# Thresholded attention with a gated mix: transposed weights copied by ScalarE or VectorE, rooms counted at creation, new due offsets

## The chip, the cores and the metric

One core of one Trainium2 chip runs the whole program. The metric is device time in microseconds (us), from start to end of one execution; lower is better. Engines are named as in the profile: PE is TensorE's matrix multiply and PEld its weight load, DVE is VectorE, ACT is ScalarE, POOL is GpSimd, SP is SyncE, which issues the DMAs.

## The reference

```
scores = q @ k.T / sqrt(64)                     # 8 batches, 8 heads, 576 x 576
keep   = scores >= max(scores, row) - tau       # tau = 0.02
attn   = exp(scores - max) where kept, else 0
attn   = attn / (sum(attn, row) + 1e-9)
x      = attn @ v, heads side by side           # 8 x 576 x 512
gate   = sigmoid(causal convolution of x, 5 taps for each channel)
out    = (gate * (x @ w_val)) @ w_out           # 512 x 512 each
```

Everything is float32. The three projection weights arrive as 64-bit words, which the kernel turns into float32 at its start.

## The kernel before

The work is cut into 32 units, one for each batch and pair of heads; four units make a batch. A unit has nine score tiles of 128 rows. In code and profile:

- **Scores** (S, L594): PE multiplies q and k into a PSUM room `u`. There are four rooms, each two banks wide, and everything that PE writes goes into one of them.
- **Row minimum** (L601): DVE scales the scores into `sb` and finds the row's extreme `nm`. It frees the PSUM room of the scores.
- **Threshold** (L609, L611), then **exp** (L619) on ACT into `e`, then **keep** (L636) on DVE, which multiplies by the mask into `pp` and sums the row. The planner can choose another way: ACT makes a steep ramp (L617) and a second exp with the sum (L630), and DVE adds 1e-9 to the sum (L656). This spares DVE the keep.
- **Reciprocal** (L657) and its spreading over 128 columns (`inv`, L665 on ACT or L667 on POOL).
- **Transposes** (T, L724): PE turns `pp` and `inv` against `ident` into a PSUM room: eight pieces (512 columns) for a group's first head, and ten and two of `inv` (768 columns) for the second. The 64 rows that are left of each head form a group of their own, `pl`.
- **Copy** (L736): the turned weights go from PSUM to `T` in SBUF, 512 or 768 columns; this frees the room. In the kernel before only ACT does it. The copies of `pl` (L740, L744) are ACT's in both kernels.
- **Attend** (C, L797; L768 in the first five units): 40 matmuls of `T` with `v`, and DVE divides them into `xT` (L774, L806).
- **Convolution** (L859, L864), **gate** (L889), and the parts of `xT` whose sum is the float32 value (`xh`, `xl`).
- **Products** (P, L955): in 16 runs of 24 matmuls a batch, 8 for `w_val` and 8 for `w_out`, after all four units of the batch. Between the two runs of a product ACT reads two numbers (`seen`, L943). The results leave by L993 (DVE) and L1057 (DVE) or L1059 (ACT).

No order is written out by hand. While the program is built, `carry_out` plans it. Each operation has an engine (or some that it may choose from), a cost in us, a due time, what it waits for and what rooms it takes. The planner takes the engine on which something can begin first, and there the operation with the smallest due time; that is then the order of the instructions in each engine's queue, which the chip carries out strictly from front to back. A due time is the number of the tile plus an offset from a table: `EARLY` before tile 69, `AT` after it. `PACE_M` is the distance in due time of one product run from the next. `FREE` names the operations that may go to a second engine from tile 69 on.

A room is a buffer in turn. `Rooms` keeps two lists: `times`, the planner's book of when rooms come free, and `free`, the buffers that are handed out when the planned instructions are emitted. The first unit takes one buffer of `pp` and one of `pl` already while the operations are being set up (`load_at_once`, L489), by `take`, which shortens `free` alone.

```
        def take(self):
            return self.free.pop(0)[1]
```

The choice between engines is a list of ways (`either`, L140). In the kernel before the copy is written with no second way in force, since `FREE` doesn't hold `copy`:

```
                    [] if self.both else either(
                        k, "copy", ("DVE", moved(m * P), moved(m * P) + 0.14, self.copy(c0, m, nc.vector.tensor_copy))
                    ),
```

Of the kernel before, what the change touches and what calls it, by code (L numbers as in the profile page):

```python
# [19 lines left out]
PACE_M = 2.32187  # L20
# [8 lines left out]
MERGED = 0.17  # L29
AT_ONCE = 4  # L30
# [3 lines left out]
for x in range(6):  # L34
# [9 lines left out]
    inv=2,  # L44
# [6 lines left out]
    swap=1421.79, fetch_q=-40.66, score=724.17, largest=2786.67, lowest=-2765.51,  # L51
    weigh=-6117.15, keep=1522.46, add=80.1, inv=-1623.91, divide=-1008.91, turn=-3930.93,
    copy=862.76, attend=-3114.29, evac=992.12, fetch=1723.48, high_k=-882.65, low_k=8.36,
    scale_q=3700.52, high_q=607.44, low_q=504.1, place=-1721.2, copies=1191.3, copies_q=1475.29,
    fetch_v=-167.12, prep=-27.65, early1=1435.43, early2=486.5, early3=169.93,
    conv_high=-4198.07, tap0=1991.9, conv_low=7462.8, tap=1501.34, tap_step=-6371.23,
    gate=-331.54, products=737.92, val=512.47, g_high=2207.99, g_low=4141.22, out=3582.59,
    send=724.8, words=-4.76, words_step=7.01, words_fetch=0.77, split=35.72, words_sub=-25.09,
    words2=-1.91, cw=-6.65, corner=-6.73,
# [3 lines left out]
    swap=-3308.32, fetch_q=-1710.45, score=-200.07, largest=2077.61, lowest=7991.15,  # L63
    weigh=-5989.81, keep=-497.79, add=34.01, inv=-769.95, divide=699.66, turn=-4372.54,
    copy=-1133.49, attend=-844.28, evac=-2380.24, fetch=1474.15, high_k=-1420.92, low_k=1798.23,
    scale_q=809.97, high_q=21.29, low_q=-257.02, place=1138.28, copies=2504.1, copies_q=3020.69,
    fetch_v=-2736.64, prep=-4.29, early1=15.1, early2=13.7, early3=23.08, conv_high=-526.99,
    tap0=3714, conv_low=5082.45, tap=-2747.74, tap_step=-4329.15, gate=839.2, products=737.34,
    val=-3061.81, g_high=1852.92, g_low=1584.46, out=-922.38, send=-3484.92, words=561.36,
    words_step=236.07, words_fetch=1847.17, split=-1153.58, words_sub=-721.5, words2=-332.82,  # L70
    cw=-3820.12, corner=3365.88,
# [3 lines left out]
FREE = ('conv_high', 'low_q', 'out')  # L75
# [3 lines left out]
def tile_thresholded_attention_gated_mix(  # L79
# [84 lines left out]
    class Rooms:  # L164
# [6 lines left out]
        def take(self):  # L171
            return self.free.pop(0)[1]
# [9 lines left out]
    shape = [0]  # L182
    wire = [1.2]
# [29 lines left out]
    def carry_out():  # L213
        done_ops = []
        while True:
            best = None
            for e, ops in open_ops.items():
# [7 lines left out]
                if can:  # L225
                    t = min(x for x, _ in can)
                    o = min((x[1] for x in can if x[0] <= t), key=lambda o: o.due)
                    if best is None or (t, o.due) < (best[0], best[1].due):
                        best = (t, o, e)
# [964 lines left out]
```

## Time and profile before

| what | value |
| --- | --- |
| median of 3 runs | 698.6 us (697.45 to 698.98) |
| the profiled execution | 697.67 us, its span 695.9 us |
| PE busy | 664.3 us, 95% of the span |
| DVE busy | 596.1 us, 86% |
| ACT busy | 587.4 us, 84% |
| POOL busy | 249.5 us, 36% |

Three stretches are to be told apart. Until about 147 us the weights are being converted beside the first units. From there to 657 us the program repeats itself with each batch: scores, transposes and attend of one batch, with the products of the batch before it in between. From 657 us on PE has little but the last batch's products. Busy shares over the whole span mix the three. A matmul's record ends where a model puts it, and matmuls overlap, so that a short wait can hide within PE's busy time: the distance from the start of one piece to the start of the next tells more than its length.

### The profile page before, as it was taken

What the parts mean: (1) busy time and instruction counts of PE and PEld (TensorE: products, weight loads), DVE (VectorE), ACT (ScalarE), POOL (GpSimd) and SP (SyncE); (2) the same over time, 40 slices, a digit from 0 to 9 for tenths busy, and PEclk for the clock granted to TensorE, in tenths of its full rate; (3) what the DMA queues carried; (4) which work ended last, traced back from release to release, by engine and by line L of the source; (5) the groups of instructions that cost most, each with busy time, mean ns of one, the idle gap of its engine ahead of it and who ended that gap; (6) DMA issues with size and microseconds to landing.
All of it is one profiled execution on the core that took longest, in us unless ns stands there. A gap on an engine that the chain in (4) does not pass through costs nothing.

```text
span 695.9 us, 21477 instructions
## 1 busy us (share of the span) xinstructions
PE 664.3 (95%) x8610; PEld 521.8 (75%) x8610; DVE 596.1 (86%) x1598; ACT 587.4 (84%) x1206; POOL 249.5 (36%) x404
## 2 busy tenths in 40 slices
PE   8877889999999999999999999999999999999997
PEld 5544557667887777888787788877778887777897
DVE  6988989998888898988979989888989889799642
ACT  6998989999889988998879989799889988799620
POOL 2554555673222620433222422226214332224231
PEclk9999999999999999999999999999999999999999
DMA  7123333023321233223222233311332232220102
GB/s 266 51 96 108 123 116 103 33 70 117 118 87 29 78 120 102 84 86 103 64 94 86 68 120 103 103 40 66 120 106 82 85 104 75 83 86 1 53 19 70
DMA packets 21076, 61.19 MB, mean 88 GB/s; under 512 B 2928, under 2 KB 4336, under 8 KB 20976
## 3 DMA queue, kind: packets, MB, share of 16 engines
q1 hardware_dynamic: 20832, 59.62, 25.3%
q8 instruction: 68, 1.11, 0.7%
q14 instruction: 32, 0.26, 0.1%
q10 hardware_dynamic: 144, 0.20, 0.1%
HBM read 50.37 MB, written 9.44 MB: 86 GB/s over the span
## 4 chain that ended last, share of the span: by engine, by line
PE 53%; DVE 27%; ACT 13%; issue 6%; DMA 0%; DVEq 0%; ACTq 0%
PE u L955 19%; PE u L797 14%; DVE sb L601 12%; PE u L594 11%; DVE pp L636 8%; PE u L724 7%; ACT e L619 3%; ACT T L736 3%; ACT pp L630 3%; PE u L768 2%; ACT e L617 2%; DVE pre L864 2%; DVE r L657 1%; DVE pl L636 1%; ACT inv L665 1%
## 5 line engine op out<-in xcount | busy, mean ns | idle before, releaser
L601 DVE TENSOR_SCALAR_CACHE_REDUCE sb<-u,sc 128x576 f32<-128x576 f32 x288 | 228.0, 809 | 26.2 <-PE u L594 13.9
L594 PE MATMUL u<-k,q 64*128 64x288 f32 x1240 | 190.0, 418 | 5.1 <-DVE sb L601 3.3
L736 ACT COPY T<-u 128x512 f32<-128x512 f32 (+1 forms) x256 | 169.9, 688 | 13.2 <-PE u L724 12.4
L636 DVE SCALAR_TENSOR_TENSOR pp<-sb,th,e 128x577 f32<-128x577 f32 x164 | 145.0, 892 | 16.1 <-ACT e L619 15.3
L619 ACT ACTIVATE e<-sb,nm 128x576 f32<-128x576 f32 x193 | 146.6, 772 | 3.5 <-DVE sb L601 1.3
L797 PE MATMUL u<-T,v 128*64 128x256 f32 (+1 forms) x1080 | 136.9, 408 | 2.0 <-ACT T L736 2.0
L724 PEld LDWEIGHTS u<-ident,pp 64*128 64x128 f32 x2304 | 102.8, 139 | 46.1 <-ACT T L736 9.8
L594 PEld LDWEIGHTS u<-k,q 64*128 64x128 f32 x1240 | 108.4, 187 | 29.5 <-DVE sb L601 8.9
L724 PE MATMUL u<-ident,pp 64*128 64x64 f32 x2304 | 114.7, 226 | 15.3 <-DVE sb L601 7.8
L797 PEld LDWEIGHTS u<-T,v 128*64 128x64 f32 x1080 | 75.1, 137 | 54.4 <-ACT T L736 3.1
L864 DVE SCALAR_TENSOR_TENSOR pre<-xT,cw,pre 128x576 f32<-128x576 f32 x121 | 107.7, 890 | 1.7 <-POOL pre L859 0.9
L955 PE MATMUL u<-xh,wvh 64*128 64x288 f32 x512 | 87.3, 326 | 0.9 <-ACT seen L943 0.3
L955 PE MATMUL u<-gh,woh 64*128 64x288 f32 x512 | 84.1, 316 | 0.9 <-ACT T L744 0.6
L617 ACT ACTIVATE e<-sb,th 128x576 f32<-128x576 f32 x95 | 73.3, 775 | 8.0 <-DVE th L611 5.3
L955 PE MATMUL u<-xh,wvl 64*128 64x288 f32 x512 | 78.7, 291 | 0.0
L955 PE MATMUL u<-xl,wvh 64*128 64x288 f32 x512 | 78.6, 291 | 0.0
L955 PE MATMUL u<-gh,wol 64*128 64x288 f32 x512 | 77.9, 291 | 0.0
L955 PE MATMUL u<-gl,woh 64*128 64x288 f32 x512 | 77.9, 291 | 0.0
L630 ACT ACTIVATE pp<-e,minus 128x576 f32<-128x576 f32 x92 | 71.2, 774 | 0.7 <-DVE pp L636 0.2
L1024 POOL TENSOR_TENSOR gl<-g,gh 128x288 fp32r<-128x288 f32 x64 | 58.9, 935 | 31.8 <-ACT gh L1016 31.6
L667 POOL TENSOR_SCALAR inv<-r 128x128 f32<-128x128 f32 x79 | 25.0, 316 | 123.8 <-DVE r L657 106.1
L955 PEld LDWEIGHTS u<-xh,wvh 64*128 64x128 f32 x512 | 51.1, 185 | 6.4 <-DVE xT L806 3.3
(92 smaller groups left out, 992.7 us busy)
## 6 DMA issues: line engine op xcount, KB each, us to landing
q<-qT SPq DMA_DIRECT2D x31, 608.0 KB, 4.1
k<-kT SPq DMA_DIRECT2D x31, 496.0 KB, 5.0
v<-vs SPq DMA_DIRECT2D x32, 320.0 KB, 2.9
outT<-o SPq DMA_DIRECT2D x28, 288.0 KB, 2.2
pre<-w_val SPq DMA_DIRECT2D x4, 512.0 KB, 6.9
pre<-w_out SPq DMA_DIRECT2D x4, 512.0 KB, 3.5
outT<-o SPq DMA_DIRECT2D x8, 144.0 KB, 1.8
pp<-first SPq DMA_DIRECT2D x2, 192.0 KB, 3.0
```

The costliest lines, as they stand in the source:

```text
L594: nc.tensor.matmul(row(self.s)[:, a, :], t.q[rows, x : x + P], t.k[rows, k0 : k0 + HS], start=i == 0, stop=h is not None or i == 1, skip_g ...
L601: nc.vector.tensor_scalar(self.sb[:, :S].rearrange("p (a f) -> p a f", a=2), row(self.room()), sc, None, op0=ALU.mult, op1=ALU.min, accum_ ...
L617: nc.scalar.activation(y, x, AF.Prelu, bias=self.th, scale=-1.0, alpha=STEEP)
L619: nc.scalar.activation(y, x, AF.Exp, bias=self.nm, scale=-1.0)
L630: nc.scalar.activation(grp.p[:, i * S : (i + 1) * S], self.e[:, :S], AF.Exp, bias=minus, accum_out=grp.sums[:, i : i + 1])
L636: nc.vector.scalar_tensor_tensor(grp.p[:, i * S : (i + 1) * S + 1], self.sb, self.th, self.e, op0=ALU.is_le, op1=ALU.mult, accum_out=grp.s ...
L724: nc.tensor.transpose(tp[:, r, i * APART_BY : i * APART_BY + D], x[rows, :], ident[rows, rows])
L736: engine(T[:, c0 : c0 + n, self.off : self.off + P].rearrange("p c (r q) -> p r c q", r=2), tp)
L797: nc.tensor.matmul(a[hs, : W[half.j]], t.v[:, c0 : c0 + D], half.T[:, 2 * NKC if c == NKC else h * NKC + c, 0 : W[half.j]], start=c == 0, ...
L864: engine.scalar_tensor_tensor(cv, pair.xT[:, i + a : i + z], cw[:, g, i : i + 1], cv, op0=ALU.mult, op1=ALU.add)
L955: nc.tensor.matmul(made["room"][:, to, 0:HS], wt[rows, c, e * P : (e + 1) * P], moving(c, i)[rows, parts[j]], start=turn == c == n == 0, s ...
L1024: engine.tensor_sub(gs[e][1][:, c], g[x][:, c], gs[e][0][:, c].bitcast(F32))
```

## The change

`take` now also shortens `times` when it is called before the planned instructions are emitted, so that the planner knows of three rooms of `pp` and one of `pl` instead of four and two. `FREE` holds `copy`, so that each copy of 512 or 768 columns from tile 69 on goes to ACT or DVE, as the planner finds; `low_q`, which it loses, names nothing in this kernel. The due offsets in `AT` and `EARLY` and `PACE_M` are other numbers. `AVOID`, a weight on the cost of going from one kind of matmul to another, is 0.0 and changes nothing.

```
-PACE_M = 2.32187
+PACE_M = 2.20003
+AVOID = 0.0
 AT = dict(
-    copy=862.76, attend=-3114.29, evac=992.12, fetch=1723.48, high_k=-882.65, low_k=8.36,
+    copy=1463.16, attend=-2397.28, evac=2111.21, fetch=2756.29, high_k=-882.65, low_k=8.36,
...
-FREE = ('conv_high', 'low_q', 'out')
+FREE = ('conv_high', 'out', 'copy')
...
         def take(self):
+            if not emitting:
+                self.times.pop(0)
             return self.free.pop(0)[1]
...
+    emitting = []
...
-                    o = min((x[1] for x in can if x[0] <= t), key=lambda o: o.due)
+                    o = min((x[1] for x in can if x[0] <= t), key=(lambda o: o.due + AVOID * CHANGE.get((shape[0], o.shape), 0.0)) if e == "PE" else lambda o: o.due)
...
+        emitting.append(True)
         for o, emit in done_ops:
```

Counted over the program, the planned instructions that change their number are these:

| instruction | engine | before | after |
| --- | --- | --- | --- |
| copy of 512 columns, L736 | ACT | 128 | 76 |
| copy of 768 columns, L736 | ACT | 128 | 88 |
| copy of 512 columns | DVE | 0 | 52 |
| copy of 768 columns | DVE | 0 | 40 |
| keep, L636 | DVE | 193 | 143 |
| second exp, L630 | ACT | 95 | 145 |
| 1e-9 to the sum, L656 | DVE | 77 | 115 |
| `inv`, L665 | ACT | 81 | 45 |
| `inv`, L667 | POOL | 79 | 115 |
| result, 576 columns, L1057 / L1059 | DVE / ACT | 7 / 21 | 12 / 16 |
| threshold, L611 / L609 | DVE / ACT | 113 / 101 | 121 / 106 |

PE has the same matmuls. Their order is the same in the first 284 rows, which end at 147.4 us in the trace of before, and in the last 259; between them it is another. The first 274 rows of DVE and 220 of ACT are the same too. In each batch from there on PE goes from transposes to scores 17 times instead of 14, from scores to products 13 times instead of 9 and from transposes to products 3 times instead of 7.

The first place is on PE, before the attend of a unit in the repeating stretch (a second unit of a batch); `u_94` to `u_97` are the four PSUM rooms, `pp_117` to `pp_119` and `pl_120` the weights to be turned. Before:

```order
L594 MATMUL u_96<-k_99,q_101 128x288 x2
L594 MATMUL u_97<-k_99,q_101 128x288 x2
L594 MATMUL u_94<-k_99,q_101 128x288 x2
L724 MATMUL u_95<-ident,pp_117 128x64 x10
L724 MATMUL u_95<-ident,inv_130 128x64 x2
L724 MATMUL u_96<-ident,pl_120 128x64 x10
L724 MATMUL u_96<-ident,inv_129 128x64 x2
L724 MATMUL u_97<-ident,pp_119 128x64 x8
L797 MATMUL u_95<-T_1_132,v_103 64x320 x10
```

After:

```order
L729 MATMUL u_95<-ident,pp_117 128x64 x10
L729 MATMUL u_95<-ident,inv_130 128x64 x2
L599 MATMUL u_96<-k_99,q_101 128x288 x2
L729 MATMUL u_97<-ident,pl_120 128x64 x10
L729 MATMUL u_97<-ident,inv_129 128x64 x2
L599 MATMUL u_94<-k_99,q_101 128x288 x2
L802 MATMUL u_95<-T_1_132,v_103 64x320 x10
```

The attend takes the room `u_95`, which is free once the weights of `pp_117` have been copied out of it; two score tiles now stand between, and the eight transposes of `pp_119` have moved behind the attend.

The second place is on ACT, before the copies of the attend one unit earlier. Before:

```order
L617 ACTIVATE e_105<-sb_107,th_115 128x576
L943 COPY seen<-u_94 128x2
L630 ACTIVATE pp_117,sums_122<-e_105,minus 128x576
L619 ACTIVATE e_104<-sb_108,nm_112 128x576
L619 ACTIVATE e_105<-sb_106,nm_109 128x576
L736 COPY T_0_133<-u_95 128x2x6x64
L740 COPY T_1_132<-u_97 128x8x64
L744 COPY T_1_132<-u_97 64x2x64 x2
```

After:

```order
L741 COPY T_0_133<-u_96 128x2x4x64
L614 ACTIVATE th_115<-nm_111,less 128x1
L670 COPY inv_129<-r_128 128x128
L622 ACTIVATE e_105<-sb_107,th_115 128x576
L635 ACTIVATE pp_117,sums_122<-e_105,minus 128x576
L741 COPY T_0_133<-u_97 128x2x6x64
L745 COPY T_1_132<-u_95 128x8x64
L749 COPY T_1_132<-u_95 64x2x64 x2
```

The copy of 768 columns that frees the attend's room stood behind two exps and a second exp; now it stands behind a ramp and a second exp.

The third place is on DVE, after the division of the unit of the first place. Before:

```order
L806 TENSOR_TENSOR xT_136<-u_95,T_1_132 128x320
L656 TENSOR_SCALAR sums_123<-sums_123 128x2
L657 RECIPROCAL r_127<-sums_123 128x2
L806 TENSOR_TENSOR xT_136<-u_95,T_1_134 128x256
L601 TENSOR_SCALAR sb_108,nm_112<-u_97,sc 128x576
L611 TENSOR_SCALAR th_116<-nm_112,less 128x1
L636 SCALAR_TENSOR_TENSOR pp_117,sums_124<-sb_108,th_116,e_104 128x577
L601 TENSOR_SCALAR sb_106,nm_109<-u_96,sc 128x576
L601 TENSOR_SCALAR sb_107,nm_110<-u_97,sc 128x576
```

After:

```order
L811 TENSOR_TENSOR xT_136<-u_95,T_1_132 128x320
L741 COPY T_0_131<-u_97 128x2x4x64
L741 COPY T_0_131<-u_94 128x2x4x64
L811 TENSOR_TENSOR xT_136<-u_95,T_1_134 128x256
L606 TENSOR_SCALAR sb_107,nm_111<-u_97,sc 128x576
L606 TENSOR_SCALAR sb_108,nm_112<-u_96,sc 128x576
L616 TENSOR_SCALAR th_116<-nm_112,less 128x1
L641 SCALAR_TENSOR_TENSOR pp_118,sums_123<-sb_107,th_115,e_105 128x577
L606 TENSOR_SCALAR sb_106,nm_109<-u_95,sc 128x576
```

Two copies now stand on DVE ahead of the row minima that free PSUM rooms of scores.

## Rows read from the trace of the kernel before

**Rows 1.** The page: busy us, share of the span and instructions.

```profile
PE 664.3 (95%) x8610; PEld 521.8 (75%) x8610; DVE 596.1 (86%) x1598; ACT 587.4 (84%) x1206; POOL 249.5 (36%) x404
```

**Rows 2.** Windows: stretch, length, busy us of PE, PEld, DVE, ACT, POOL, clock, DMA.

```profile
0.00:147.00 147.00, 126.60 (x1394) 86.15 (x1394) 130.64 (x379) 130.80 (x257) 74.43 (x102) 0.97 0.33 114
147.00:657.00 510.00, 503.65 (x6750) 404.28 (x6748) 451.22 (x1195) 449.48 (x930) 165.87 (x292) 1.00 0.25 83
657.00:696.00 39.00, 34.02 (x472) 31.33 (x470) 14.20 (x26) 7.12 (x21) 9.15 (x11) 0.99 0.14 51
25.00:100.00 75.00, 61.98 (x664) 39.57 (x662) 68.57 (x194) 69.19 (x134) 36.08 (x48) 0.93 0.27 89
374.13:455.18 81.05, 80.14 (x1075) 64.42 (x1072) 72.24 (x193) 71.23 (x148) 25.54 (x47) 1.00 0.27 89
```

**Rows 3.** Waits from 147 to 657 us: us in total, times, longest.

```profile
DVE pp L636 <- ACT e L619: 14.0, 27, 0.9
...
PE u L797 <- ACT T L736: 2.0, 5, 0.4
...
PE u L724 <- DVE sb L601: 1.5, 6, 0.2
```

**Rows 4.** Timeline of PE: an attend that doesn't wait; start, length, what.

```profile
394.00 0.53 PE L724 MATMUL u<-ident,pl 64*128 64x64 f32 x10
...
394.82 0.49 PE L797 MATMUL u<-T,v 128*64 128x320 f32 x2
```

**Rows 5.** Timeline of PE: the attend of the second place, which waits.

```profile
432.99 0.48 PE L724 MATMUL u<-ident,pl 64*128 64x64 f32 x10
...
434.17 0.76 PE L797 MATMUL u<-T,v 128*64 128x320 f32 x4 [0.39 <-ACT T L736]
```

**Rows 6.** Timeline of ACT: what stands before that copy.

```profile
432.01 1.43 ACT L619 ACTIVATE e<-sb,nm 128x576 f32<-128x576 f32 x2
433.34 0.78 ACT L736 COPY T<-u 128x768 f32<-128x768 f32 x1
```

**Rows 7.** Timeline of PE: the attend of the first place, which waits too.

```profile
451.91 1.63 PE L594 MATMUL u<-k,q 64*128 64x288 f32 x12
453.36 0.48 PE L724 MATMUL u<-ident,pp 64*128 64x64 f32 x10
453.67 0.24 PE L724 MATMUL u<-ident,inv 64*128 64x64 f32 x2
...
455.18 0.49 PE L797 MATMUL u<-T,v 128*64 128x320 f32 x2
```

**Rows 8.** Timeline of PE: scores between transposes, twelve and then four.

```profile
445.39 1.68 PE L594 MATMUL u<-k,q 64*128 64x288 f32 x12
446.90 0.41 PE L724 MATMUL u<-ident,pp 64*128 64x64 f32 x8
...
449.16 0.71 PE L594 MATMUL u<-k,q 64*128 64x288 f32 x4
449.97 0.46 PE L724 MATMUL u<-ident,pp 64*128 64x64 f32 x8
```

**Rows 9.** Groups by line and shape, whole span: busy us, mean ns of one, idle before.

```profile
L736 ACT COPY T<-u 128x768 f32<-128x768 f32 x128 | 101.1, 790 | 11.4 <-PE u L724 11.4
L736 ACT COPY T<-u 128x512 f32<-128x512 f32 x128 | 74.8, 586 | 1.8 <-PE u L724 0.9
L1057 DVE TENSOR_SCALAR o<-u 128x576 f32<-128x576 f32 x7 | 5.3, 758 | 3.2 <-PE u L955 2.8
L1057 DVE TENSOR_SCALAR o<-u 128x288 f32<-128x288 f32 x8 | 3.5, 455 | 9.5 <-PE u L955 6.4 <-DMA outT<-o 3.1
L636 DVE SCALAR_TENSOR_TENSOR pp<-sb,th,e 128x577 f32<-128x577 f32 x164 | 145.0, 892 | 16.1 <-ACT e L619 15.3
L656 DVE TENSOR_SCALAR sums<-sums 128x1 f32<-128x1 f32 x59 | 8.6, 146 | 1.4 <-ACT pp L630 1.3
L630 ACT ACTIVATE pp<-e,minus 128x576 f32<-128x576 f32 x92 | 71.2, 774 | 0.7 <-DVE pp L636 0.2
```

More of the change, by code (lines that the diff above doesn't have):

```diff
@@ L50 @@
 AT = dict(
-    swap=1421.79, fetch_q=-40.66, score=724.17, largest=2786.67, lowest=-2765.51,
-    weigh=-6117.15, keep=1522.46, add=80.1, inv=-1623.91, divide=-1008.91, turn=-3930.93,
-    copy=862.76, attend=-3114.29, evac=992.12, fetch=1723.48, high_k=-882.65, low_k=8.36,
+    swap=972.96, fetch_q=-565.68, score=723.13, largest=3245.52, lowest=-2958.04,
+    weigh=-6617.16, keep=2505.12, add=80.1, inv=-2476.71, divide=-1209.34, turn=-4906.96,
+    copy=1463.16, attend=-2397.28, evac=2111.21, fetch=2756.29, high_k=-882.65, low_k=8.36,
     scale_q=3700.52, high_q=607.44, low_q=504.1, place=-1721.2, copies=1191.3, copies_q=1475.29,
[L55 to L58, printed above, removed]
+    fetch_v=-61.82, prep=-27.65, early1=1692.46, early2=1012.74, early3=418.6,
+    conv_high=-4588.42, tap0=2444.55, conv_low=7206.43, tap=1107.3, tap_step=-6154.55,
+    gate=162.76, products=737.48, val=763.41, g_high=2913.83, g_low=4335.82, out=3826.38,
+    send=1334.54, words=-4.76, words_step=7.01, words_fetch=0.77, split=35.72, words_sub=-25.09,
     words2=-1.91, cw=-6.65, corner=-6.73,
@@ L62 @@
 EARLY = dict(
-    swap=-3308.32, fetch_q=-1710.45, score=-200.07, largest=2077.61, lowest=7991.15,
-    weigh=-5989.81, keep=-497.79, add=34.01, inv=-769.95, divide=699.66, turn=-4372.54,
-    copy=-1133.49, attend=-844.28, evac=-2380.24, fetch=1474.15, high_k=-1420.92, low_k=1798.23,
+    swap=-3657.6, fetch_q=-3182.83, score=-525.18, largest=2042.6, lowest=7744.8,
+    weigh=-6155.64, keep=70.07, add=34.01, inv=-98.37, divide=692.58, turn=-4190.93,
+    copy=-1403.92, attend=-673.12, evac=-1722.8, fetch=1828.89, high_k=-1420.92, low_k=1798.23,
     scale_q=809.97, high_q=21.29, low_q=-257.02, place=1138.28, copies=2504.1, copies_q=3020.69,
[L67 to L71, printed above, removed]
+    fetch_v=-2948.37, prep=-4.29, early1=15.1, early2=13.7, early3=23.08, conv_high=-1097.69,
+    tap0=3007.84, conv_low=5373.03, tap=-2468.49, tap_step=-3639.3, gate=743.17,
+    products=738.57, val=-2569.18, g_high=1905.59, g_low=2404.82, out=-695.1, send=-3725.48,
+    words=609.07, words_step=289.44, words_fetch=1437.37, split=-617.28, words_sub=-529.86,
+    words2=-477.38, cw=-4772.29, corner=3365.88,
 )
```

## The prediction

> **What bounds the kernel now.** The page comes first: PE is busy for 95% of the span, DVE for 86% and ACT for 84% [rows 1]. An average over a start, a repeating middle and an end says little, so the windows come next [rows 2]. From 25 to 100 us PE is busy for 62.0 of 75 us, and DVE (68.6) and ACT (69.2) hold it up. From 147 to 657 us PE is busy for 503.65 of 510 us: here PE sets the pace, DVE has 451.2 and ACT 449.5 us. From 657 us on PE does the last batch's products. One batch of the middle, from attend to attend, takes 81.05 us with PE busy for 80.14, DVE for 72.24 and ACT for 71.23 [rows 2].
>
> So a change in the middle can win only what PE waits for there, and the third view is what it waits for. In the open, that is 510 − 503.65 = 6.35 us. The list of waits says for what [rows 3]: the attend for a copy by ACT, 2.0 us in five places, and the transposes for a row minimum on DVE, 1.5 us in six; the rest is scattered. More hides behind records that overlap, so I read PE's timeline by starts. An attend that doesn't wait starts 0.82 us after the 20 transposes ahead of it began [rows 4]. The attend at 434.17 starts 1.18 us after its 20 [rows 5]: it waited 0.36 us, and the timeline of ACT shows why. The copy that frees its PSUM room began at 433.34, when two exps had ended [rows 6]. The attend at 455.18 starts 1.82 us after its 32 transposes [rows 7]; ten transposes take 0.31 us there (453.36 to 453.67), so twelve more than 20 account for 0.37 us, and 1.82 − 0.82 − 0.37 = 0.63 us is waiting. The first kind comes five times and the second six times in the trace: 5 × 0.36 + 6 × 0.63 = 5.6 us. Two of a batch's four attends wait, the two others don't.
>
> **The change part by part.** The start and the end. On PE the first 284 rows, up to 147 us, and the last 259 are in the same order as before, so the 147 us of the start and the 39 us of the end stay as they are: nothing. Only the 510 us between are planned anew, 510 / 81.05 = 6.3 batches.
>
> The count of rooms. The planner believed in one room of `pp` and one of `pl` too many. On the chip this could only show as a keep or a second exp that waits for PE to give a room back. The list of waits of the middle names 14.0 us of keeps that wait for ACT's exp [rows 3], and no keep or second exp that waits for PE. The correction by itself is worth nothing. Its price can't be negative there; if the tighter book made the plan delay a keep, it would cost a wait of the size of those 27, about 0.5 us at a place.
>
> The copies. 52 of 512 columns and 40 of 768 go from ACT to DVE. ACT loses 52 × 0.586 + 40 × 0.790 = 62.1 us, but gets 50 second exps of 0.774 (38.7 us) in return, and gives 36 `inv` to POOL [rows 9]. DVE's price for a copy isn't in the trace. The nearest row is the result's, also from PSUM to SBUF in float32: 758 ns for 576 columns and 455 for 288, so 1.05 ns a column and 152 ns fixed [rows 9]. That gives 691 ns for 512 and 960 ns for 768 columns, 52 × 0.691 + 40 × 0.960 = 74.3 us. The low end is ACT's own price, 62.1 us. I take 74.3, since it comes from the same engine. DVE loses 50 keeps of 0.892 us (44.6 us), and gains 38 additions of 1e-9 (38 × 0.146 = 5.5 us), five results (5 × 0.758 = 3.8 us) and some small ones, about 1.7 us. In sum DVE gets some 41 us more in the middle, 41 / 6.3 = 6.5 us a batch: 78.7 us busy where 72.2 were. None of it lies on PE's path as long as PE's rooms come free in time; PE hides it. If that cover goes, DVE sets the pace (a rival, below).
>
> [...]
>
> What the move buys is a second server for PSUM rooms. At the second place of the section on the change, the attend's room waited for a copy behind two exps; now the copy stands behind a ramp and a second exp, with some copies taken off that queue. At the first place the room's copy had the time of 12 + 8 transposes, about 0.6 us, before the attend; now two score tiles and twelve transposes stand between, at 0.12 us a matmul (1.45 us for twelve [rows 7]) some 0.5 + 0.4 + 0.5 = 1.4 us, more than a copy's 0.79. All four attends of a batch are now such that their room's copy has from 1.1 to 1.7 us by this count. The bounds for these waits are 5.6 us won and nothing won. I take two thirds, 3.7 us: the order removes the cause, but one of the four places has little room to spare, and an ACT queue that runs late by one exp (0.77 us) brings the wait back.
>
> The other waits in the open, 6.35 − 2.0 − 1.5 = 2.85 us, are spread over many places. A new order takes some away and makes others; bounds 2.85 us won and as much lost. I take half of it as won, 1.4 us, because an operation now finds two engines for a copy.
>
> The order on PE. A going over from transposes to scores has a price: twelve scores take 1.51 us between transposes [rows 8] and 1.45 us behind products [rows 7], 0.06 us. There are 17 of them in a batch instead of 14: 3 × 0.06 × 6.3 = 1.1 us lost. For the other goings over no rows stand apart from waits; at 0.06 us for each of the 4 fewer from transposes to products and the 4 more from scores to products they cancel, and I take nothing, ± 1.5 us.
>
> `PACE_M` 2.20 for 2.32. 16 runs a batch now claim 16 × 2.20 = 35.2 of the 36 tiles' due times where they claimed 37.1, so products come earlier among the scores. PE is full either way, and the end of the program begins with the same 18 runs of products in both orders: nothing.
>
> The DMAs. SP issues the same transfers with a few exchanged in order. None of the waits of PE, DVE or ACT in the middle [rows 3] is for a DMA: nothing.
>
> The sum: −3.7 − 1.4 + 1.1 = −4.0 us. On the profiled execution, 697.67 us, that gives 693.7. That execution lies 0.9 us under the median of three, 698.6, so against the median I predict 694.6.
>
> **The rivals.** *All waits go.* If both kinds of wait vanish, −5.6 − 2.85 + 1.1 = −7.4 us, 691.2. More is hidden: four scores between transposes take 0.81 us at 449.16 [rows 8], where four of the twelve there take 0.50; six such places would give 1.9 us more, 689.3. For it speaks that the new order repeats itself from batch to batch as the old one does, so that what is gained once is gained six times. Against it, no engine has as much to spare as before.
>
> *The waits only move.* The attends no longer wait, but scores and transposes do, because the row minima that free their rooms now stand behind copies on DVE (the third place). Then PE's excess is as large as it was: 698.6, from 697.2 to 700.0. For it speaks that the four PSUM rooms are the same, and DVE's queue holds longer pieces.
>
> *DVE becomes the bound.* With 78.7 us a batch DVE would be busy for 97% of 81.05 us. In the stretch where DVE and ACT hold PE up, it is busy for 91.4% (68.57 of 75 us) [rows 2]. It works in order, and a copy whose transposes aren't done yet holds back the row minimum behind it; ACT's copies idled 11.4 us for that reason [rows 9]. If DVE can't pass 95%, a batch takes 82.8 us, 1.8 more, and the time is 698.6 + 6.3 × 1.8 = 710; at 91.4% it would be 86.1 us a batch and 730. The point from which it decides is 78.7 / 81.05: it costs from the first 0.1 us on that DVE must idle more than 2.3 us in a batch. Against it: durations overstate DVE, since one instruction starts before the record of the last ends, and 62.1 us for the copies instead of 74.3 would leave 4.2 us of idle time. At its mild end it is 701.
>
> **How the numbers follow.** The forecast, some of the waits gone (691.5 to 697), has 0.46. All waits gone: 0.12. Waits only moved: 0.20. DVE the bound: 0.22, of which a third at its mild end under 702. A measurement of this kernel can tell 0.2%, 1.4 us, from no change. The first two are faster, 0.58; the third is the same, 0.20; the last is slower, 0.22. The predicted time is the forecast's, 694.6. The range reaches from the hidden waits' end, 689.3, to the mild end of the DVE bound, 702: it leaves out most of that case, about 0.15, and little below.
>
> **What would show it.** Right: the distance between attends of successive batches falls from 81.05 to about 80.4 us; the attend's wait for a copy by ACT (2.0 us) leaves the list; attends start 0.8 to 1.0 us after their last 20 transposes; DVE's share in the middle rises to 95% or more with copies of 0.69 and 0.96 us, and ACT's falls. Wrong: transposes and scores of PE wait for row minima or copies of DVE for more than 6 us in the middle, and the batch takes 81 us or more; or the first 147 us differ, which I hold for the same.

## The result and the profile after

The changed kernel takes 703.47 us (median of 6 runs, 702.02 to 706.01) where the kernel before takes 698.79 (6 runs beside it): a ratio of 1.0071, 95% interval 1.0043 to 1.0098. It is slower by 4.7 us; 694.6 was predicted, with 702.0 as the upper end. Lines of the changed kernel stand five lower in its code (L601 is L606, L636 is L641, L656 is L661, L724 is L729, L736 is L741, L955 is L960).

The page of the changed kernel, busy times, to be read against [rows 1], and its chain of work that ended last:

```profile
PE 664.8 (95%) x8610; PEld 524.8 (75%) x8610; DVE 634.3 (91%) x1641; ACT 565.6 (81%) x1173; POOL 258.7 (37%) x432
...
DVE 51%; PE 32%; issue 8%; ACT 6%; DMA 2%; SPq 1%; DVEq 0%; ACTq 0%
```

The chain of the kernel before:

```profile
PE 53%; DVE 27%; ACT 13%; issue 6%; DMA 0%; DVEq 0%; ACTq 0%
```

PE's busy share hasn't moved, but the chain has: it runs over DVE for half of the span instead of a quarter.

To see where the 4.4 us between the two spans (695.88 and 700.25) lie, I cut both at three starts of an attend: the first attend of L797 (L802 after the change), the one six batches later, and the last, two units further on. Windows of the kernel before, then of the changed one (stretch, length, busy time of PE, PEld, DVE, ACT and POOL, clock, DMA):

```profile
131.54:617.26 485.72, 478.56 (x6383) 382.04 (x6381) 431.44 (x1149) 429.55 (x889) 162.16 (x280) 1.00 0.27 89
617.26:656.85 39.59, 39.49 (x543) 32.59 (x541) 33.46 (x85) 33.44 (x69) 13.79 (x23) 1.00 0.06 20
656.85:695.88 39.03, 34.17 (x474) 31.48 (x472) 14.35 (x26) 7.17 (x21) 9.15 (x11) 1.00 0.15 52
```

```profile
131.32:620.09 488.77, 479.54 (x6372) 384.49 (x6369) 462.37 (x1182) 410.68 (x860) 170.05 (x306) 1.00 0.26 88
620.09:661.20 41.11, 40.51 (x555) 33.44 (x553) 39.21 (x95) 31.06 (x66) 14.86 (x24) 1.00 0.06 20
661.20:700.25 39.05, 34.16 (x474) 31.49 (x472) 14.33 (x26) 7.18 (x21) 9.14 (x11) 0.99 0.15 52
375.53:457.04 81.51, 80.36 (x1075) 64.76 (x1073) 77.63 (x199) 68.31 (x145) 26.95 (x50) 1.00 0.27 88
```

The start (131.5 and 131.3 us) and the end (39.03 and 39.05) are the same. Six batches take 3.05 us more, 0.5 us each, and the stretch over the last three attends 1.5 us more. The last row is the batch of [rows 2]: 81.51 where 81.05 stood, with DVE busy for 77.63 us where 72.24 stood.

Waits from 147 to 657 us in the changed kernel (us in total, times, longest):

```profile
PEld u L960 <- DVE sums L661: 5.1, 12, 0.6
...
PE u L599 <- DVE T L741: 2.1, 6, 0.4
...
PE u L729 <- DVE sb L606: 1.8, 6, 0.6
...
DVE pp L641 <- ACT e L624: 0.5, 1, 0.5
```

The attend's wait for a copy by ACT (2.0 us in [rows 3]) has gone, as forecast, and so have the keeps' waits for an exp (14.0 us). Among the releasers stand DVE's copies and row minima now, and the `sums` of L661, which are the additions of 1e-9 (a weight load, PEld, that waits can still lie behind PE's work: at the place below PE's scores of L599 run from 388.35 to 389.54). That last name misleads. DVE and PEld at one of the twelve places:

```profile
388.67 0.69 DVE L741 COPY T<-u 128x512 f32<-128x512 f32 x1
389.27 0.15 DVE L661 TENSOR_SCALAR sums<-sums 128x1 f32<-128x1 f32 x1
389.41 0.19 PEld L960 LDWEIGHTS u<-xh,wvh 64*128 64x128 f32 x2 [0.33 <-DVE sums L661]
```

At all twelve the weight load starts 0.05 us after a copy on DVE has ended and just before the addition ends. So the products wait for the copy, which frees a PSUM room. The run without additions, below, has the same twelve waits under the copy's name:

```profile
PEld u L957 <- DVE T L738: 4.3, 12, 0.6
```

Groups of the changed kernel over the whole span (busy us, mean ns of one, idle before):

```profile
L741 DVE COPY T<-u 128x768 f32<-128x768 f32 x40 | 38.0, 950 | 0.2
L741 DVE COPY T<-u 128x512 f32<-128x512 f32 x52 | 35.1, 683 | 0.0
...
L661 DVE TENSOR_SCALAR sums<-sums 128x1 f32<-128x1 f32 x85 | 12.4, 145 | 0.4 <-ACT pp L635 0.4
...
L661 DVE TENSOR_SCALAR sums<-sums 128x2 f32<-128x2 f32 x30 | 8.9, 296 | 0.1
```

The copies cost what the prediction had worked out from the results' rows (960 and 691 ns).

### The profile page after: what moved, and what is told of

Same layout as the page of the kernel before. It is cut to its first block, busy times and chain, and to the rows that moved or that the text cites. A ratio compares the mean times of both kernels' runs of the same rounds, so it can differ in the third digit from the quotient of the medians.

```text
span 700.2 us, 21509 instructions
## 1 busy us (share of the span) xinstructions
PE 664.8 (95%) x8610; PEld 524.8 (75%) x8610; DVE 634.3 (91%) x1641; ACT 565.6 (81%) x1173; POOL 258.7 (37%) x432
## 4 chain that ended last, share of the span: by engine, by line
DVE 51%; PE 32%; issue 8%; ACT 6%; DMA 2%; SPq 1%; DVEq 0%; ACTq 0%
DVE sb L606 16%; PE u L960 13%; DVE pp L641 10%; PE u L599 8%; DVE T L741 7%; DVE pre L869 7%; PE u L802 6%; PE u L729 4%; DVE g L998 2%; DVE r L662 2%; DVE xT L811 2%; ACT e L624 2%; DVE th L616 2%; DMA pre<-w_val 1%; PE u L773 1%
## 5 line engine op out<-in xcount | busy, mean ns | idle before, releaser
L606 DVE TENSOR_SCALAR_CACHE_REDUCE sb<-u,sc 128x576 f32<-128x576 f32 x288 | 227.5, 809 | 15.6 <-PE u L599 11.7
L599 PE MATMUL u<-k,q 64*128 64x288 f32 x1240 | 194.6, 423 | 10.7 <-DVE sb L606 5.0
L802 PE MATMUL u<-T,v 128*64 128x256 f32 (+1 forms) x1080 | 136.9, 408 | 0.1
L599 PEld LDWEIGHTS u<-k,q 64*128 64x128 f32 x1240 | 108.3, 189 | 33.8 <-DVE sb L606 9.1
L729 PEld LDWEIGHTS u<-ident,pp 64*128 64x128 f32 x2304 | 98.9, 139 | 40.3 <-ACT T L741 10.5
L641 DVE SCALAR_TENSOR_TENSOR pp<-sb,th,e 128x577 f32<-128x577 f32 x132 | 123.3, 937 | 3.0 <-ACT e L624 1.8
L622 ACT ACTIVATE e<-sb,th 128x576 f32<-128x576 f32 x145 | 111.9, 774 | 16.6 <-DVE th L616 9.3
L729 PE MATMUL u<-ident,pp 64*128 64x64 f32 x2304 | 108.7, 225 | 14.0 <-ACT T L741 6.8
L741 ACT COPY T<-u 128x512 f32<-128x512 f32 (+1 forms) x164 | 110.5, 692 | 7.0 <-PE u L729 6.3
L802 PEld LDWEIGHTS u<-T,v 128*64 128x64 f32 x1080 | 75.2, 137 | 54.3 <-issue 2.6
L624 ACT ACTIVATE e<-sb,nm 128x576 f32<-128x576 f32 x143 | 109.5, 770 | 4.3 <-DVE pp L641 1.9
L869 DVE SCALAR_TENSOR_TENSOR pre<-xT,cw,pre 128x576 f32<-128x576 f32 x121 | 103.8, 858 | 2.0 <-POOL pre L890 0.9
L635 ACT ACTIVATE pp<-e,minus 128x576 f32<-128x576 f32 x124 | 95.7, 772 | 1.3 <-DVE pp L641 0.2
L672 POOL TENSOR_SCALAR inv<-r 128x128 f32<-128x128 f32 x115 | 35.3, 307 | 152.0 <-DVE r L662 100.1
L960 PE MATMUL u<-xh,wvh 64*128 64x288 f32 x512 | 87.8, 331 | 0.8 <-ACT seen L948 0.3
L960 PE MATMUL u<-gh,woh 64*128 64x288 f32 x512 | 85.9, 323 | 0.9 <-ACT seen L948 0.3
L960 PE MATMUL u<-gl,woh 64*128 64x288 f32 x512 | 78.0, 292 | 0.0
L960 PE MATMUL u<-gh,wol 64*128 64x288 f32 x512 | 78.0, 291 | 0.0
L960 PE MATMUL u<-xl,wvh 64*128 64x288 f32 x512 | 77.9, 292 | 0.0
L960 PE MATMUL u<-xh,wvl 64*128 64x288 f32 x512 | 77.9, 292 | 0.0
L741 DVE COPY T<-u 128x768 f32<-128x768 f32 (+1 forms) x92 | 72.5, 799 | 0.2
```

The costliest lines, as they stand in the source:

```text
L599: nc.tensor.matmul(row(self.s)[:, a, :], t.q[rows, x : x + P], t.k[rows, k0 : k0 + HS], start=i == 0, stop=h is not None or i == 1, skip_g ...
L606: nc.vector.tensor_scalar(self.sb[:, :S].rearrange("p (a f) -> p a f", a=2), row(self.room()), sc, None, op0=ALU.mult, op1=ALU.min, accum_ ...
L622: nc.scalar.activation(y, x, AF.Prelu, bias=self.th, scale=-1.0, alpha=STEEP)
L624: nc.scalar.activation(y, x, AF.Exp, bias=self.nm, scale=-1.0)
L635: nc.scalar.activation(grp.p[:, i * S : (i + 1) * S], self.e[:, :S], AF.Exp, bias=minus, accum_out=grp.sums[:, i : i + 1])
L641: nc.vector.scalar_tensor_tensor(grp.p[:, i * S : (i + 1) * S + 1], self.sb, self.th, self.e, op0=ALU.is_le, op1=ALU.mult, accum_out=grp.s ...
```

## Experiments

The theories. **Load**: DVE with the copies is too full, whatever it is filled with. **Additions**: the planner now chooses the second exp 50 times more, which brings 38 more additions of 1e-9 (115 for 77), and these cost far more than the 0.146 us that I gave them. **Order**: the new due offsets make a worse order. Each ratio below is to runs of the kernel before on the same chip, whose medians were 698.0 to 698.8 us.

### Less and more load on DVE

Two runs let DVE do half of each convolution tap from tile 69 on, in the changed kernel and in the one before:

```
-                cv = batch.pre[:, g, a:z]
+                m = (z - a) // 2 if k >= EARLY_UNTIL else z - a
+                cv = batch.pre[:, g, a : a + m]
```

> The changed kernel with its order untouched; from tile 69 on each convolution tap on VectorE works on half of its columns, so half of the convolution is left out. 16 taps a batch of 0.85 us become about 0.5: VectorE's work falls by some 5.5 us a batch, away from the rooms of PSUM. Theory A (VectorE's load of 77.6 of 81.5 us a batch slows the kernel): the 4.7 us come back, 698 to 699.5 us, and the batch falls to 81.0 us. Theory B (the new order itself, three rooms of transposes behind each attend that wait for their copies, whoever is busy): 702 to 704 us, a batch stays at 81.4 to 81.5 us.

> The kernel before with the same half taps from tile 69 on (half of the convolution is left out). VectorE has 9 us to spare in a batch there. Theory A and theory B both: PE sets the pace, within 1.5 us of the kernel before, 698 to 699.5 us. If it falls by more than 2 us, VectorE held PE up in the kernel before as well.

Measured: 695.5 us after the change (ratio to the kernel before 0.9965, 0.9952 to 0.9977) and 695.65 before it (0.996, 0.9945 to 0.9975). The first is 8.0 us less than the changed kernel, the second 2.4 us less than the kernel before. A batch of the changed kernel with half taps:

```profile
374.12:454.21 80.09, 79.52 (x1074) 64.74 (x1072) 72.74 (x199) 68.17 (x145) 26.36 (x50) 1.00 0.28 90
```

With DVE back at 72.7 us a batch the loss is gone, so DVE holds the changed kernel up. (Not all of the gain need be load: the six long additions of a section below last only 0.2 us in this run, and 0.3 us with half copies.) That the kernel before gains as well says that PE didn't hide all of DVE there either.

The third run halves the columns of the copies on DVE alone:

```
+                    h = D if engine == nc.scalar.copy else D // 2
+                    engine(to[..., 0:h], tp[..., 0:h])
```

> The changed kernel with its order untouched; the 92 copies on VectorE move half of their columns (the other half of these weights is left stale): 0.42 and 0.55 us instead of 0.68 and 0.95, so VectorE's work falls by 28 us in all, 4.5 a batch, and the rooms that these copies hold come free 0.27 to 0.4 us earlier. Theory A: like the half taps, 698 to 699.5 us. Theory B: the waits behind the attends (0.51, 0.61 and 0.25 us a batch) shrink by 0.3 each, about 5 us in all, 697 to 700 us. If it is faster than the half taps by over 2 us, the time for which a room is held counts more than the load.

Measured: 695.9 us (0.9969, 0.9959 to 0.9979), 7.6 us less than the changed kernel. The fourth gives the kernel before more load, an instruction on 256 columns behind each tap (some 0.5 us each):

```
+                if k >= EARLY_UNTIL:
+                    x, y = (lane.whole[:, 0:256] for lane in lanes)
+                    nc.vector.scalar_tensor_tensor(y, x, cw[:, g, i : i + 1], y, op0=ALU.mult, op1=ALU.add)
```

> The kernel before with its order untouched, and behind each convolution tap on VectorE from tile 69 on another one of 256 columns on tiles that nobody reads: 16 x about 0.4 = 6 us more a batch for VectorE, about what the change gives it (5.4). Theory A: VectorE comes to 78 us of a batch of 81 and the kernel slows like the changed one, 702 to 706 us. Theory B: VectorE's spare time takes it, 698.5 to 701 us.

Measured: 718.12 us (1.0292, 1.0274 to 1.0309). The batch:

```profile
374.00:458.66 84.66, 81.39 (x1076) 64.54 (x1075) 78.00 (x209) 71.44 (x148) 25.33 (x46) 1.00 0.26 85
```

A batch takes 3.6 us more for 5.8 us more of DVE, and DVE is busy for 92% of it, when the changed kernel has it at 95% (77.63 of 81.51). So no one busy share at which DVE "becomes the bound" fits both. When a piece of work comes in the queue must count too; these runs don't show how much. All four moved further than either theory had it: 2.5, 2.4 and 1.1 us under the nearest range with half taps after the change, half taps before it and half copies, and 12 us over it with more load.

### Without the additions

```
-                if self.bent:
-                    x = self.sums[:, self.bent[0] : self.bent[-1] + 1]
-                    nc.vector.tensor_scalar(x, x, 1e-9, None, op0=ALU.add)
                 nc.vector.reciprocal(self.r[:, 0:n], self.sums[:, 0:n])
```

By the reference the row's largest score has the weight exp(0) = 1, so a sum is at least 1, and 1e-9 is lost in float32.

> The changed kernel, its order untouched, without the additions of 1e-9 on VectorE (L661): a sum holds the term exp(0) = 1 of its row's largest score, and 1e-9 added to 1 or more leaves a float32 as it is, so nothing is lost. In the trace of the changed kernel these additions take VectorE 0.22 to 0.33 us from start to start, about 23 us from 147 to 657 us, 3.5 us a batch. Theory A (VectorE's load): the half taps took 4.9 us a batch off and won 8.0 us, so this wins about 5: 697.5 to 700 us. Theory B (the order, not the load): 702 to 704 us.

> The kernel before, its order untouched, without the same additions: 9 a batch of 0.19 us, 1.7 us a batch. Half taps took 4.3 us a batch off VectorE and won 2.4 us, so by the load this wins about 1: 696.5 to 698 us. If it wins as much as in the changed kernel, the additions cost by their latency (sum, reciprocal, spread, transposes) and not by the load.

Measured: 687.91 us for the changed kernel (0.9854, 0.9833 to 0.9875) and 690.45 for the one before (0.989, 0.9872 to 0.9907). That is 9.6 and 6.0 us under the lowest that was expected: the additions cost far more than their load. They cost 15.6 us after the change and 7.6 us before it. The difference, 8 us, is more than the whole loss, and without them the changed kernel is the faster one by 2.5 us; it is the fastest version of this study, 10.1 us under the kernel before. The windows of both without additions, the kernel before first:

```profile
128.91:610.52 481.61, 475.01 (x6383) 382.75 (x6380) 424.84 (x1095) 428.41 (x889) 162.77 (x280) 1.00 0.27 90
610.52:649.60 39.08, 38.98 (x543) 32.38 (x540) 32.67 (x80) 33.32 (x69) 14.11 (x23) 1.00 0.06 21
```

```profile
128.77:608.22 479.45, 473.93 (x6372) 383.06 (x6369) 451.14 (x1091) 408.86 (x860) 167.28 (x306) 1.00 0.27 90
608.22:648.69 40.47, 40.11 (x555) 33.25 (x553) 37.96 (x89) 31.03 (x66) 14.64 (x24) 1.00 0.06 20
```

Here is what the change does without its side effect: six batches are 2.2 us shorter, and the stretch over the last three attends, whose order is new too, gives 1.4 us back. (These two executions lie 0.9 us apart, the medians 2.5, so the windows tell where rather than how much.) The first row of each also shows that the additions cost 2.6 us before the first attend of this kind, in both kernels.

Why an addition is dear is seen at one place of DVE's queue. The timeline of DVE in the changed kernel, between two row minima (start, length, what):

```profile
386.13 0.15 DVE L661 TENSOR_SCALAR sums<-sums 128x1 f32<-128x1 f32 x1
386.39 0.17 DVE L662 RECIPROCAL r<-sums 128x2 f32<-128x2 f32 x1
386.47 0.80 DVE L606 TENSOR_SCALAR_CACHE_REDUCE sb<-u,sc 128x576 f32<-128x576 f32 x1
```

The same place without additions:

```profile
379.04 0.16 DVE L659 RECIPROCAL r<-sums 128x2 f32<-128x2 f32 x1
379.12 0.80 DVE L606 TENSOR_SCALAR_CACHE_REDUCE sb<-u,sc 128x576 f32<-128x576 f32 x1
```

The reciprocal, for which nothing behind it on DVE waits, holds the queue for 0.08 us, start to start. It needs the addition's result itself and starts 0.26 us after the addition. So the row minimum behind, which frees a PSUM room, comes 0.26 us later, and so does everything behind it; the record's 0.145 us shows little more than half.

This place is one of the dear ones. Without the long additions of the next section, the reciprocal starts 0.17 to 0.20 us after its addition in 51 of 108 cases and 0.24 to 0.27 us in 57. By the trace's semaphores the 51 wait for one and the 57 for two; in the kernel before, 71 wait for one and take 0.17 to 0.20 us, and 5 for two and take 0.25 to 0.27.

### Six long additions

One place of each of six batches is worse. DVE and, below it, POOL in the changed kernel:

```profile
407.04 0.65 DVE L661 TENSOR_SCALAR sums<-sums 128x2 f32<-128x2 f32 x1
407.72 0.17 DVE L662 RECIPROCAL r<-sums 128x2 f32<-128x2 f32 x1
407.81 0.80 DVE L606 TENSOR_SCALAR_CACHE_REDUCE sb<-u,sc 128x576 f32<-128x576 f32 x1
...
409.27 0.95 DVE L741 COPY T<-u 128x768 f32<-128x768 f32 x1
```

```profile
406.93 0.73 POOL L851 TENSOR_TENSOR xl<-xT,xh 128x256 fp32r<-128x256 f32 x1
408.06 0.30 POOL L672 TENSOR_SCALAR inv<-r 128x128 f32<-128x128 f32 x1 [0.39 <-DVE r L662]
```

The addition ends when POOL's subtraction does (407.69 and 407.66), and the row minimum, the copy and POOL's `inv` are late with it. PE there, in the changed kernel and then without additions:

```profile
407.58 0.66 PE L599 MATMUL u<-k,q 64*128 64x288 f32 x4
408.07 0.48 PE L729 MATMUL u<-ident,pp 64*128 64x64 f32 x10
408.41 0.28 PE L729 MATMUL u<-ident,inv 64*128 64x64 f32 x2
408.67 1.24 PE L599 MATMUL u<-k,q 64*128 64x288 f32 x8
409.74 0.41 PE L729 MATMUL u<-ident,pp 64*128 64x64 f32 x8
410.28 0.41 PE L960 MATMUL u<-gh,woh 64*128 64x288 f32 x2
```

```profile
400.72 0.47 PE L726 MATMUL u<-ident,pp 64*128 64x64 f32 x10
401.02 0.23 PE L726 MATMUL u<-ident,inv 64*128 64x64 f32 x2
401.09 1.20 PE L599 MATMUL u<-k,q 64*128 64x288 f32 x8
402.11 0.41 PE L726 MATMUL u<-ident,pp 64*128 64x64 f32 x8
402.33 0.39 PE L957 MATMUL u<-gh,woh 64*128 64x288 f32 x2
```

From the ten transposes to the products it is 2.21 us (408.07 to 410.28) and 1.61 without additions (400.72 to 402.33): 0.6 us at one place, of the 1.7 us that the additions cost this batch (81.51 to 79.83, from attend to attend). The late `inv` has little part in it: from the ten transposes to those of `inv` it is 0.34 us and 0.30. But 0.2 us more pass before the eight scores, which start when the row minimum has ended (408.61), and 0.3 us more before the products, which start when the copy on DVE has ended (410.22).

Over the whole trace 30 additions have two columns; the seven of them that start while a POOL instruction of two inputs (TENSOR_TENSOR) runs last 0.65 to 1.24 us, the other 23 don't pass 0.17. Of the 85 with one column 16 start beside such an instruction, and none is longer than 0.15 us. The kernel before has one long addition, at 100 us, where the changed kernel has its seventh. Why two columns are held up and one isn't, the traces don't show.

So one run makes each addition on one column alone (the second column of those 30 groups stays without it):

```
-                    x = self.sums[:, self.bent[0] : self.bent[-1] + 1]
+                    x = self.sums[:, self.bent[0] : self.bent[0] + 1]
```

> The changed kernel with all 115 additions of 1e-9 at their places, each on one column alone (in the 30 groups with two such columns the second stays without it). If the seven long additions cost what they last (six of about 0.5 us more than a short one and one of 1.1 us, 4 us in all) and reach the end: 699 to 701 us. If they are hidden, or if waiting for GpSimd isn't what makes them long: 702.5 to 704 us.

Measured: 700.52 us (1.003, 1.0016 to 1.0045), 2.95 us less than the changed kernel with as many additions (0.3 to 5 us by the spread of the runs, an estimate). So the long additions do reach the end. All 115 last 145 ns in the mean:

```profile
L661 DVE TENSOR_SCALAR sums<-sums 128x1 f32<-128x1 f32 x115 | 16.7, 145 | 0.4 <-ACT pp L635 0.4
```

### The count of additions, and nothing else

The kernel before gets 38 additions more, its order unchanged, and the changed kernel loses 38 (every third):

```
+                elif plain.append(1) or len(plain) * 38 % 83 < 38:
+                    x = self.sums[:, 0:1]
+                    nc.vector.tensor_scalar(x, x, 1e-9, None, op0=ALU.add)
```

```
-                if self.bent:
+                if self.bent and (plain.append(1) or len(plain) % 3 != 0):
```

> The kernel before, its order unchanged, with 38 additions of 1e-9 more (115, as many as after the change), spread over the reciprocals that had none. Theory (the further additions are the loss): 38 times 0.10 to 0.14 us, 3.8 to 5.3 us more than the kernel before, 702 to 704 us. Rival (they cost only beside the copies on VectorE): within 1.5 us of the kernel before, 698 to 700 us.

> The changed kernel, its order unchanged, with every third addition of 1e-9 left out, so 77 of the 115 stand, as many as before the change. Theory: 38 times 0.136 us, 5.2 us less than the changed kernel, 697 to 699.5 us, no longer slower than the kernel before. Rival (the copies' load costs): 702 to 703.5 us.

Measured: 703.3 us (1.0077, 1.0058 to 1.0096) and 696.12 us (0.9974, 0.996 to 0.9988). The kernel before, with the changed kernel's count, is as slow as the changed kernel; the changed kernel, with the count of before, is faster than the kernel before by 1.9 us. The rival, that additions cost only beside the copies, expected 698 to 700 and 702 to 703.5 us, and both measurements speak against it. A batch of the middle shows that DVE's busy time by itself isn't the reason either, in the kernel before with 38 more and then in the changed kernel with 38 fewer:

```profile
377.67:459.20 81.53, 80.37 (x1076) 64.13 (x1073) 72.73 (x198) 71.60 (x148) 25.53 (x47) 1.00 0.27 88
```

```profile
374.45:454.74 80.29, 79.67 (x1075) 64.63 (x1073) 76.66 (x194) 68.19 (x145) 26.61 (x50) 1.00 0.27 89
```

The first takes as long as the changed kernel's batch (81.51) with 4.9 us less of DVE; the second has DVE busy for 95% like it and takes 1.2 us less. The two runs don't move exactly the 38 that the change brought: five of those added and seven of those left out lie before 147 us, where both kernels have the same. Those left out hold six of the seven long ones, and those added, all on one column, none.

Two more runs vary what an addition is. In the one it works on a tile of its own, so that the reciprocal doesn't wait for it; in the other it is made twice, the second waiting for the first:

```
-                    x = self.sums[:, self.bent[0] : self.bent[-1] + 1]
+                    x = spare[:, self.bent[0] : self.bent[-1] + 1]
```

> The changed kernel with all 115 additions at their places in VectorE's queue, but on a tile of their own, so that the reciprocal behind waits for none of them. If an addition costs by the time that it holds the queue: 15.6 us times some 0.08 of 0.145 us (one small instruction that nothing waits for takes 0.08 us of the queue) is 8 to 9 us over the kernel without additions, 695 to 698 us. If it costs by the wait of the reciprocal alone: 688 to 690 us. If any instruction there costs as much: 702 to 704 us.

> The changed kernel with each of its 115 additions of 1e-9 made twice, the second waiting for the first. If the price of one stays at 0.136 us: 15.6 us more than the changed kernel, 717 to 721 us. If it grows, since VectorE then sets the end more often: up to 115 times 0.25 us, 725 to 732 us. If it falls, since the wait of the reciprocal is already paid: 708 to 714 us.

Measured: 693.89 us (0.9944, 0.9924 to 0.9965) and 724.3 us (1.0373, 1.0346 to 1.0399); each falls into the gap between two of the ranges. Apart, the addition holds the queue for 0.07 us and the reciprocal follows at once:

```profile
380.10 0.15 DVE L663 TENSOR_SCALAR spare<-spare 128x1 f32<-128x1 f32 x1
380.17 0.16 DVE L664 RECIPROCAL r<-sums 128x2 f32<-128x2 f32 x1
```

All additions apart cost 6.0 us over none, the true ones 15.6: more than half of the price is the wait for a result. (The seven long ones stay long in this run, 0.71 to 1.25 us, so the 6.0 us hold them.) As far as one batch shows, most of it reaches PE by the queue and not by the later `inv`: of the 1.7 us of the batch above, compared start by start with the run without additions, about 1.2 us arise ahead of scores and products, which read no `inv`, and 0.2 us ahead of the transposes of `inv`. The price of one, from the medians:

| kernel | additions | us | us for each |
| --- | --- | --- | --- |
| before | 0 to 77 | 690.45 to 698.05 | 0.099 |
| before | 77 to 115 | 698.02 to 703.3 | 0.139 |
| after | 0 to 77 | 687.91 to 696.12 | 0.107 |
| after | 77 to 115 | 696.12 to 703.47 | 0.193 |
| after | 115 to 230 | 703.47 to 724.3 | 0.181 |

By the spread of the runs the rows of 38 are good to some 0.03 to 0.04 us and the others to 0.02 (an estimate). Six of the seven long additions are among the 38 in the fourth row. At 2.95 us for seven they are 2.5 of its 7.35 us, and 4.8 us are left for 38, 0.13 each, close to the second row.

### Half of the change alone

The list of free operations of after with the offsets of before, and the other way round, each with additions and without:

```
-FREE = ('conv_high', 'low_q', 'out')
+FREE = ('conv_high', 'out', 'copy')
```

> The kernel before with the changed list of free operations ('conv_high', 'out', 'copy') and its own due offsets: its planner gives VectorE 105 of the copies of transposed weights and, choosing the second exponential more often, 108 additions of 1e-9 (77 before, 115 after the change). Theory (the additions are the loss, 0.10 to 0.14 us each): 31 more of them cost 3 to 4 us against a relief of 2 to 4 us from the copies, 697 to 702 us. Rival (the copies' load on VectorE is the loss, and 105 of them are more than the 92 of the changed kernel): 703 to 707 us. Rival (the new due offsets are the loss): 694 to 697 us.

> The same, without the additions of 1e-9. Theory: 108 times 0.10 to 0.14 us less than with them, 11 to 15 us, so 685 to 690 us, and no slower than the kernel before without its additions (690.45 us). Rival (the copies' load): slower than 690.45 by the 4 us that the changed kernel lost, 694 to 697 us. Rival (the offsets): 685 to 688 us, and the loss of the changed kernel stands in the next two runs.

> The changed kernel with the list of free operations of before ('conv_high', 'low_q', 'out'): all copies of transposed weights are ScalarE's again, the new due offsets stay, and 87 additions of 1e-9 stand on VectorE. Theory (the additions): ten more than before cost 1 to 1.4 us, and offsets that were found for another set of free operations may cost some more, 698 to 702 us. Rival (the copies' load): 696 to 699 us, since no copy is on VectorE. Rival (the offsets): 703 us or more.

> The same, without the additions of 1e-9. Theory: 87 times 0.10 to 0.14 us less than with them, 9 to 12 us, so 688 to 692 us. Rival (the copies' load): near 688 us as well, but then the two kernels with copies on VectorE and without additions must be slower than this one. Rival (the offsets): 693 us or more, slower than the kernel before without its additions.

Measured: 729.92 us (1.0451, 1.0425 to 1.0478), 715.73 (1.0244), 728.23 (1.042, 1.0399 to 1.0442) and 716.77 (1.0261). All theories missed these by far. The additions cost 14.2 us for 108 and 11.5 us for 87, 0.13 each, as elsewhere; but without any of them both halves are 25 to 29 us slower than either whole. Windows of the middle with additions, the list alone first, then the offsets alone:

```profile
147.00:657.00 510.00, 485.98 (x6328) 379.29 (x6330) 476.88 (x1188) 412.79 (x874) 149.33 (x253) 1.00 0.25 82
```

```profile
147.00:657.00 510.00, 483.72 (x6352) 383.08 (x6348) 425.54 (x1126) 428.17 (x883) 168.84 (x295) 1.00 0.25 82
```

PE idles for 24 and 26 us where 6.35 stood [rows 2], in the one with DVE busy for 94%, in the other for 83%. So neither half can be priced by itself: offsets are found for one set of choices, and an order from offsets of another set is worse by more than all that is at stake here. These runs don't say which places lose it.

### A tap for GpSimd

GpSimd is busy for 37% of the span, so the last tap was given to it, as two instructions, in both kernels without additions:

```
+                if i == KT - 1 and k >= EARLY_UNTIL:
+                    tmp = r_tmp.free[0][1]
+                    nc.gpsimd.tensor_scalar(
+                        tmp, pair.xT[:, i + a : i + z], cw[:, g, i : i + 1], 0.0, op0=ALU.mult, op1=ALU.add)
+                    nc.gpsimd.tensor_add(cv, cv, tmp)
+                    return
```

> The changed kernel without the additions, and from tile 69 on the last tap of each convolution by two instructions of GpSimd (multiply into a spare tile, add) instead of one of VectorE: nothing is left out. VectorE loses another 4 x 0.85 = 3.4 us a batch, 7 in all, more than the half taps took; GpSimd gets 4 x 2.4 = 9.5 us a batch on top of 27 of 81. Theory A: as fast as the half taps, 694.5 to 697 us, if the gate's later start (1.6 us) stays hidden behind the products, and 698 to 701 us if it does not.

> The kernel before with both: VectorE loses 1.7 + 3.4 = 5.1 us a batch, a little more than with half taps. Theory A: 695 to 697 us; slower than that only by the gate's later start.

Measured: 696.56 us (0.9973, 0.9958 to 0.9988) and 698.94 (1.0004, 0.9992 to 1.0017), 8.6 and 8.5 us more than without the move. DVE is relieved, and ACT waits instead (first with the changed kernel's order, whole span):

```profile
ACT pre L897 <- POOL pre L870: 34.0, 25, 2.4
...
L870 POOL TENSOR_TENSOR pre<-pre,tmp 128x576 f32<-128x576 f32 x25 | 37.5, 1501 | 64.2 <-DVE r L659 39.3 <-DVE pre L872 24.9
```

The gate stands in ACT's queue ahead of exps; it now waits up to 2.4 us for an addition of 1.5 us on GpSimd, and holds them back.

## Why the prediction was wrong, point by point

- **The 38 additions and the cover: the step that failed.** The sum put the additions in as "38 × 0.146 = 5.5 us" of DVE and then at nothing in the time, by "None of it lies on PE's path as long as PE's rooms come free in time; PE hides it." The 38 cost 7.4 us of the end's time after the change and 5.3 before it: the cover wasn't there. Their load was too small as well. The record's length leaves out that the reciprocal behind waits for the result; counted from start to next start over the program, the 115 hold DVE's queue for 29.1 us and the 77 of the kernel with 38 fewer for 18.0, so 11 us for 38.
- **PE hides DVE.** The kernel before shows that this didn't hold there either: half taps gain 2.4 us in it, and half copies 7.6 us after the change. PE's share of 99% in the middle [rows 2] was taken for slack on DVE's side. DVE's 58.8 us of idle time (510 − 451.2) aren't spare, because PE waits for a row minimum or a copy that comes late (1.5 and, for ACT's copies, 2.0 us in the open [rows 3]).
- **The copies.** Their durations, 683 and 950 ns, and DVE's load in a batch, 77.6 us, came as worked out (691, 960 and 78.7).
- **The attends' waits.** They have gone from the list, as forecast. With as many additions as before the change gives 1.9 us, without any 2.5, where −4.0 was forecast: the direction was right, the size about half. In the six batches without additions the gain is 2.2 us. The stretch over the last three attends loses 1.4 us. The prediction had looked at the order of the end, behind the last attend, and that stayed; this stretch ahead of it wasn't looked at. The other terms of the sum, 1.4 us won from scattered waits and 1.1 us lost by PE's order, no run tells apart.
- **The start, the end, the rooms.** Right: 131.5 and 131.3 us, 39.03 and 39.05. Built without the new count of rooms, the planner makes the same order on PE, DVE and ACT, so that edit does nothing here.
- **The rivals.** "DVE becomes the bound" was right in kind and named the right engine, and its mild end, 701, is near the time. Its mechanism, a share that DVE can't pass, is not what happens: 95% after the change in 81.51 us, 92% with the added load in 84.66. Nor do the copies hold back what stands behind them by waiting for their transposes: DVE idled 0.2 us before all 92. "The waits only move" was right too, for the transposes, scores and products that wait for DVE now. Of the two signs of being wrong that belong together, the batch came (81.51 us); the waits of transposes and scores for row minima and copies of DVE are 4.3 us in the open, not over 6.

## What to carry to other kernels

Price a small instruction in an engine's queue by the distance of the starts around it, with and without it, and look whether the next one needs its result: the record's length says neither. When a planner changes its choices, count every instruction that comes along with the new choice, and take the whole of it into the sum before anything is called hidden; then ask whether it is needed at all. Offsets that were found for one set of choices can't be judged with another, so undoing half of such a change tells little about the other half.

## What the runs showed of the hardware that was not expected

- A reciprocal on DVE that needs the result of the small addition ahead of it starts 0.17 to 0.20 us after it when it waits for one semaphore, and 0.24 to 0.27 us after it when it waits for two (51 and 57 cases after the change, 71 and 5 before it). Behind an addition that it doesn't need, in the run with the additions apart, it starts 0.06 to 0.08 us after it (106 of 108).
- A DVE addition on two columns that starts while a GpSimd instruction of two inputs runs lasts until that one ends (seven of seven, 0.65 to 1.24 us, with their ends 0.02 to 0.03 us apart); on one column it doesn't (none of 16).
- In the kernel before with an instruction more behind each tap, 5.8 us more of DVE in a batch where DVE had 8.8 us of idle time cost 3.6 us.
